# A hand-laid order of pieces and table of engines, laid anew: block-causal attention, routed attention and a gated MLP on one core

## The chip, the cores and the metric

The kernel runs on one core of one Trainium2 chip. A core has a matrix engine (TensorE, in profiles PE, with PEld for the loads of its weights), a vector engine (VectorE, DVE), a scalar engine (ScalarE, ACT), a general engine (GpSimd, POOL) and a sync engine (SyncE, SP) that mostly issues DMAs. Each engine takes its instructions from a queue of its own, in the order in which they were written, and waits at semaphores for what other engines make. The metric is the device time in microseconds (us) of one execution. Of the kernel before there are three timed runs, 936.07, 938.05 and 939.17 us, with a median of 938.05 us.

## The reference

For eight batches of 576 rows the reference runs three layers, one behind the other:

```
scores = q @ k^T / 8                     # 8 heads of 64 columns
scores = where(block_i >= block_j, scores, -1e9)      # blocks of 64
x = softmax(scores) @ v                  # (576, 512) for each batch

logits = x @ w_gate                      # 4 experts, the best 2 for each row
for e in range(4):
    q, k, v = x @ wq[e], x @ wk[e], x @ wv[e]
    a = softmax(causal(q @ k^T / 8))
    out += weight_of_e_in_this_row * (a @ v @ wo[e])

h = relu(out @ w_in)                     # 1024 columns
u, v = h[:, :512], h[:, 512:]
v_n = (v - mean(v)) / sqrt(var(v) + 1e-6)
y = (u * (w_spatial @ v_n + b_spatial)) @ w_out
```

## The kernel before, in words

**Tiles.** The 576 rows of a batch lie as four blocks of 128 rows and one of 64. Attention works on pairs of heads (four pairs a batch) or pairs of experts (two a batch), so a pair is named by batch and number: (0,4) is the first pair of experts of batch 0, (1,2) the third pair of heads of batch 1. Every matrix that TensorE multiplies is a pair of float16 tensors, a high part and what is left over, made by a cast (`copy16`, L350 to L357) or a scaled cast (`split16`, L233 to L239) and a subtraction. A product is then three matmuls.

**Steps of a pair.** *lq* and *lv* load q, k and v (L257 to L274). *mg* takes largest magnitudes for the scale (ACT L295 or DVE L297), *pq* and *pv* split q, k and v. *sc* has four parts: matmuls (L393 to L411), a row maximum (DVE L414, L416), a small step that makes the bias of the exponential (ACT L424 or DVE L426), and the exponentials (ACT L430, L435). *w* has three parts, and each casts the exponentials to float16 (ACT L352, DVE L354 or POOL L356) and subtracts (DVE L451 or POOL L455). *wt* is a transposing DMA on SP's queue (L460) that puts the result into the tile `pT`, *av* multiplies it with v on PE (L470) and takes the reciprocal of the sums (DVE L486, L488; L491 for a pair of experts), and *x* scales the product (DVE L499), casts and subtracts again (L504) and transposes (L506).

**Steps of a batch.** From x come the experts' q, k, v and logits (*proj* L804 to L817, *vproj* L827 to L836), the choice of two experts (*gate* L843 to L864, tiny DVE operations), pairs 4 and 5, and then the MLP: *hv* (L883 to L893), *norm0* and *norm* (L898 to L929), *gu* and *gs* (the two factors of the gate, L964 to L987), *outp*, *last* and *outp4* (L998 to L1027). *norm* has a part for each of five row blocks: one scales and shifts the block (L921, DVE or POOL), ACT casts it (L924, L926), and DVE or POOL subtracts (L929).

**Setting up.** Once, before batch 0 reaches its experts: *ldA* loads the experts' weights, *ldB* w_spatial and b_spatial in nine DMAs (L606 to L616), *ldwo* the matrix wo (L706), and w_in and w_out are converted, multiplied and split.

**What sets the order.** All of this is some 1,366 named steps, each a Python generator that is cut into pieces at its `yield`s. The tuple ORDER (from L1037) lists step numbers, and each appearance of a number issues the next piece of that step, on whatever engines the piece uses. So one list sets the order in all five queues at once. The table WAYS (from L1213) says for a place, and for each batch in turn (the last entry holds for the batches behind it), which engine a piece uses: D for DVE, A for ACT, G for POOL, S for SP's queue. Of two letters the first is the cast and the second the subtraction:

```
for i in ORDER:
    t = named[i]
    ...
    run(t)
```

Nothing else decides on time: waits are semaphores on data and on buffers (four double banks of PSUM, `duo`; four tiles each of `pf`, `p` and `pT`; eight of x).

## Time and profile before

| | |
|---|---|
| timed runs | 936.07, 938.05, 939.17 us, median 938.05 |
| the profiled execution | 931.44 us, its span 929.7 us |
| mean granted clock of TensorE | 0.962 |
| PE busy | 838.6 us (90%) |
| DVE busy | 754.4 us (81%) |
| ACT busy | 632.9 us (68%) |
| POOL busy | 547.5 us (59%) |

The profile is that of one execution, 6.61 us below the median of the timed runs. Busy time counts instructions that compute or, on POOL, issue DMAs. Where DVE is busy for nearly all of a stretch in which PE is not, what DVE has to do sets the pace there, and the rows of PE say in brackets how long it sat idle ahead of an instruction and what ended that.

### The profile page before, as it was taken

The numbers are of one execution on the slowest core, as the hardware profiler recorded it, in microseconds if no ns is written. First come the engines' busy times: TensorE is split into PE (matmuls) and PEld (weight loads), VectorE is DVE, ScalarE is ACT, GpSimd is POOL, SyncE is SP. The second block draws the span as 40 slices with busy tenths as digits, with TensorE's granted clock in tenths as the row PEclk, the third lists the DMA queues.
The fourth block names the chain that finished last, engine by engine and source line by source line (L and its number), as shares of the span: only waits on it lengthen the run. The fifth ranks groups of instructions, "written<-read, shape, count | busy, mean of one in ns | idle before, by whom it ended". The sixth has DMA issues, their size and how long they took to land. (4 is left out here: it accounts for less than half of the span.)

```text
span 929.7 us, 25206 instructions
## 1 busy us (share of the span) xinstructions
PE 838.6 (90%) x10038; PEld 616.4 (66%) x10038; DVE 754.4 (81%) x1608; ACT 632.9 (68%) x1151; POOL 547.5 (59%) x542
## 2 busy tenths in 40 slices
PE   3677887789998999989999999989999999999987
PEld 2466765567766767666776677567767786667554
DVE  6999989988998688887988799788997879468351
ACT  3867687866778777785776697675698568448232
POOL 6557457756677767785675867345857665425120
PEclk9777999599999999999999999999999999999999
DMA  9999889998789798999799799879699939914601
GB/s 202 217 220 191 185 178 177 193 158 133 164 152 201 112 186 149 197 189 169 137 159 197 133 149 199 145 138 181 139 180 171 158 58 155 202 30 77 140 1 57
DMA packets 470716, 143.66 MB, mean 155 GB/s; under 512 B 456003, under 2 KB 462499, under 8 KB 470598
## 3 DMA queue, kind: packets, MB, share of 16 engines
q1 hardware_dynamic: 461750, 129.72, 78.4%
q0 software_dynamic: 5232, 11.44, 4.9%
q8 instruction: 79, 1.29, 0.5%
q10 hardware_dynamic: 3616, 0.89, 0.5%
q14 instruction: 39, 0.32, 0.1%
HBM read 38.19 MB, written 9.44 MB: 51 GB/s over the span
## 5 line engine op out<-in xcount | busy, mean ns | idle before, releaser
L455 POOL TENSOR_TENSOR p<-pf,p 128x512 f16<-128x512 f32 (+1 forms) x198 | 242.5, 1247 | 74.7 <-DVE p L354 24.8
L414 DVE TENSOR_REDUCE st<-duo 128x2 f32<-128x1024 f32 (+2 forms) x192 | 151.2, 814 | 17.5 <-PE duo L401 8.8
L470 PEld LDWEIGHTS <-pT 128*128 128x128 f16 x4320 | 144.6, 99 | 28.2 <-DMA pT<-p 12.9
L435 ACT ACTIVATE pf<-duo,st,es 128x512 f32<-128x512 f32 (+3 forms) x224 | 122.4, 617 | 17.0 <-DVE st L426 14.2
L393 PE MATMUL duo<-qk 64*128 64x256 f16 (+3 forms) x1152 | 110.9, 315 | 20.6 <-DVE qk L239 7.7
L356 POOL TENSOR_SCALAR p<-pf 128x1024 f16<-128x1024 f32 (+1 forms) x68 | 78.0, 1149 | 86.5 <-ACT pf L435 55.9
L980 PE MATMUL duo<-wsp,vn 128*128 128x288 f16 x832 | 111.9, 286 | 2.1 <-ACT pf L435 1.1
L470 PE MATMUL duo<-v,pT 128*128 128x65 f16 (+1 forms) x2880 | 102.3, 196 | 10.2 <-DMA pT<-p 5.4
L804 PE MATMUL duo<-x,wqk 128*128 128x288 f16 x768 | 98.7, 286 | 2.1 <-DVE pf L499 0.7
L980 PEld LDWEIGHTS <-vn 128*128 128x128 f16 x832 | 80.0, 98 | 24.0 <-DVE vn L929 1.6
L804 PEld LDWEIGHTS <-wqk 128*128 128x128 f16 x768 | 74.3, 98 | 21.9 <-issue 2.9
L998 PE MATMUL duo<-wo,gT 128*128 128x512 f16 x384 | 86.0, 379 | 0.2 <-POOL gT L987 0.2
L393 PEld LDWEIGHTS <-qk 64*128 64x128 f16 x1152 | 46.2, 98 | 52.5 <-issue 33.0
L921 POOL TENSOR_SCALAR vf<-vf,nw 128x512 f32<-128x512 f32 (+1 forms) x27 | 25.8, 963 | 82.7 <-DVE nw L912 36.6
L435 ACT ACTIVATE pf<-duo,st,mt 128x256 f32<-128x256 f32 (+3 forms) x128 | 69.8, 617 | 5.3 <-DVE st L426 4.0
L451 DVE TENSOR_TENSOR p<-pf,p 128x1024 f16<-128x1024 f32 (+1 forms) x45 | 64.6, 1436 | 6.1 <-ACT p L352 5.8
L998 PEld LDWEIGHTS <-gT 128*128 128x128 f16 x384 | 36.6, 98 | 43.3 <-DVE gT L987 1.0
L504 POOL TENSOR_TENSOR xh<-pf,xh 128x640 f16<-128x640 f32 x30 | 44.8, 1494 | 32.9 <-ACT xh L352 26.6
L827 PE MATMUL duo<-wvg,x 128*128 128x260 f16 x480 | 56.5, 274 | 0.6 <-DVE nw L912 0.6
L352 ACT CAST p<-pf 128x1024 f16<-128x1024 f32 (+1 forms) x53 | 56.7, 1072 | 0.5
L470 PE MATMUL duo<-V,pT 128*128 128x65 f16 (+1 forms) x1440 | 49.6, 194 | 7.8 <-DMA pT<-p 5.2
L883 PE MATMUL duo<-wf,x 128*128 128x512 f16 x240 | 54.5, 379 | 1.8 <-DMA x<-xh 1.2
(273 smaller groups left out, 1732.2 us busy)
## 6 DMA issues: line engine op xcount, KB each, us to landing
out_dram<-pf SPq DMA_DIRECT2D x16, 512.0 KB, 3.3
nat<-in_q_dram SPq DMA_DIRECT2D x40, 128.0 KB, 3.2
nat<-in_k_dram SPq DMA_DIRECT2D x40, 128.0 KB, 3.2
wf<-in_moe_w_in_dram SPq DMA_DIRECT2D x8, 512.0 KB, 5.3
nat<-in_v_dram SPq DMA_DIRECT2D x32, 128.0 KB, 3.0
nat<-in_v_dram POOLq DMA_DIRECT2D x30, 128.0 KB, 4.6
nat<-in_q_dram POOLq DMA_DIRECT2D x22, 128.0 KB, 4.4
nat<-in_k_dram POOLq DMA_DIRECT2D x22, 128.0 KB, 4.4
```

The costliest lines, as they stand in the source:

```text
L352: A.copy(hi, src)
L356: G.tensor_scalar(hi, src, 1.0, 1.0, op0=OP.mult, op1=OP.mult)
L393: T.matmul(ph[:, hh, o:o + w], p.q[hs, a, ts], p.k[hs, bb, 0:w], start=i == 0, stop=False)
L414: V.reduce_max(st[:, 0, 2 * c:2 * c + 2], ph[:, :, off[c]:off[c] + P * (c + 1)], axis=AX.X)
L435: A.activation(pf[:, n * hh + off[c]:n * hh + off[c] + w], ph[:, hh, off[c]:off[c] + w], AF.Exp, bias=st[:, 1, 2 * c + hh:2 * c + hh + 1], ...
L451: V.tensor_sub(lo, src, hi)
L455: G.tensor_sub(lo[:, z:z + m], src[:, z:z + m], hi[:, z:z + m])
L470: T.matmul(ps[:, hh, o:o + n], pT[:, col(t, kk):col(t, kk) + P], p.v[:, hh, kk, a:a + n], start=kk == 0 and i == 0, stop=kk == nk - 1 and ...
L804: T.matmul(ps[:, MID + a:MID + a + w], wqk16[:, l, c, 2 * n + i, :], x16[c][:, r, a:a + w], start=m == 0, stop=m == 11)
L827: T.matmul(ps[:, i, :260], x16[d][:, l, P * c:P * c + P], wvg16[:, r, d, :], start=m == 0, stop=m == 11)
L980: T.matmul(ps[:, MID + a:MID + a + n], l, wsp16[:, r, c, a:a + n], start=i == 0, stop=i == 13)
L998: T.matmul(ps[:, i], gT[:, x, d, P * c:P * c + P], wo16[:, y, d, :], start=m == 0, stop=m == 11)
```

## The change

Only ORDER and WAYS differ. The same steps with the same operands are issued in another order, and some pieces go to another engine. Of ORDER a line tells nothing by itself (50 is a step's number):

```diff
-        50, 54, 54, 50, 51, 50, 50, 50, 54, 50, 50, 52, 142, 142, 142, 143, 143, 51, 54, 54, 143, 143, 143, 143, 54,
+        50, 54, 54, 51, 50, 50, 50, 50, 54, 50, 50, 52, 142, 142, 142, 143, 143, 51, 143, 54, 143, 143, 54, 54, 54,
...
-        "last": ("A", "G", "G", "G", "G", "G", "A", "D"), "lq.0": ("A", "S", "S", "S", "G", "S", "S", "G"),
+        "last": ("A", "G", "G", "G", "G", "G", "A", "G"), "lq.0": ("A", "S", "S", "S", "S", "S", "S", "G"),
...
-        "lq.3": ("S", "G", "S", "G", "G", "G", "S"), "lv.0": ("A", "G", "S", "S", "S", "S", "G"),
+        "lq.3": ("S", "G", "S", "G", "G", "G", "S"), "lv.0": ("A", "G", "G", "S", "G", "S", "G", "S"),
...
-        "mg.0.1": ("D", "A"), "mg.1.0": ("D", "D", "A", "A", "A", "D", "A", "D"),
+        "mg.0.1": ("A",), "mg.1.0": ("D", "D", "A", "D", "A", "D", "A", "D"),
...
-        "sc.5.3": ("D", "A", "D", "D", "A", "D", "D", "A"), "su.ldA": ("S",), "su.ldB": ("S",), "su.ldwo": ("G",),
+        "sc.5.3": ("D", "A", "D", "D", "A", "D", "A"), "su.ldA": ("S",), "su.ldB": ("G",), "su.ldwo": ("S",),
...
-        "w.4.0": ("AG", "GG", "DG", "DD", "GG", "DG", "DD", "DG"),
+        "w.4.0": ("AG", "GG", "AG", "DD", "GG", "GG", "AD", "AG"),
...
-        "x.1": ("DD", "DD", "GG", "GD", "GG", "AG", "GG", "GD"),
+        "x.1": ("DD", "GG", "GG", "GG", "GG", "AG", "GG", "AD"),
...
```

Over the whole program DVE has 1,597 instructions instead of 1,610, ACT 1,108 instead of 1,101, POOL 560 instead of 547 and SP 436 instead of 440. PE has the same 19,441, in an order in which mostly neighbours have changed places. On DVE there are 6 fewer magnitudes of a 128x640 tile (L297) and 5 fewer casts of 1,024 columns (L354).

**The start, POOL and SP.** The nine loads of *ldB* go from SP's queue to POOL's, and *ldwo* from POOL's to SP's. On POOL these rows stand behind the loads of v in the order before (the `p` rows are the casts and subtractions of pairs (0,0) and (0,1)):

```order
L274 DMA nat<-in_v_dram 64x2x64 x2
L356 TENSOR_SCALAR p_142<-pf 128x1024
L455 TENSOR_TENSOR p_142<-pf,p_142 128x512 x2
L356 TENSOR_SCALAR p_142<-pf 128x1088
L455 TENSOR_TENSOR p_142<-pf,p_142 128x544 x2
L235 TENSOR_SCALAR v<-nat,scb 128x10x64
L455 TENSOR_TENSOR p_142<-pf,p_142 128x512 x2
L706 DMA V_146<-in_moe_wo_dram 128x2x512
L455 TENSOR_TENSOR p_142<-pf,p_142 128x512 x2
```

And in the order of the change:

```order
L609 DMA wspb<-in_moe_w_spatial_dram 128x576
L356 TENSOR_SCALAR p_142<-pf 128x1024
L611 DMA wspb<-in_moe_w_spatial_dram 64x576
L455 TENSOR_TENSOR p_142<-pf,p_142 128x512 x2
L356 TENSOR_SCALAR p_142<-pf 128x1088
L455 TENSOR_TENSOR p_142<-pf,p_142 128x544 x2
L606 DMA wspa<-in_moe_w_spatial_dram 128x3x64
L609 DMA wspb<-in_moe_w_spatial_dram 128x64
L235 TENSOR_SCALAR v<-nat,scb 128x10x64
L611 DMA wspb<-in_moe_w_spatial_dram 64x64
L616 DMA wspb<-in_moe_b_spatial_dram 1x16x36 x3
L455 TENSOR_TENSOR p_142<-pf,p_142 128x512 x4
```

Four loads (L611 and three of L616) now stand between the split of v (L235) and the subtractions of pair (0,1), where there were none, the other five stand ahead of and between the pieces of pair (0,0), and L706 is gone. On SP's queue the stretch with the transposes of the first two pairs reads, before:

```order
L606 DMA wspa<-in_moe_w_spatial_dram 128x3x64
L460 DMA_TRANSPOSE pT<-p_142 128x16x128
L531 DMA wf_171<-in_moe_w_in_dram 128x4x512
L609 DMA wspb<-in_moe_w_spatial_dram 128x64
L611 DMA wspb<-in_moe_w_spatial_dram 64x64
L616 DMA wspb<-in_moe_b_spatial_dram 1x576 x2
L460 DMA_TRANSPOSE pT<-p_142 128x18x128
L616 DMA wspb<-in_moe_b_spatial_dram 1x576
L460 DMA_TRANSPOSE pT<-p_142 128x16x128 x2
L460 DMA_TRANSPOSE pT<-p_142 128x18x128
```

and in the change:

```order
L595 DMA wg<-in_moe_w_gate_dram 128x4x4
L460 DMA_TRANSPOSE pT<-p_142 128x16x128
L531 DMA wf_171<-in_moe_w_in_dram 128x4x512
L460 DMA_TRANSPOSE pT<-p_142 128x18x128
L706 DMA V_146<-in_moe_wo_dram 128x2x512
L460 DMA_TRANSPOSE pT<-p_142 128x16x128 x2
L460 DMA_TRANSPOSE pT<-p_142 128x18x128
```

The transposes of pair (0,1) no longer have loads of *ldB* between them, and one load of wo stands there in their place.

**The end of batch 0's heads, DVE and POOL.** In this stretch the last pairs of heads of batch 0, its experts' first pair (0,4) and the first pairs of batch 1 are in work together. On DVE, before (L499 is the product of *x* of pair (1,1), `xh` its cast and subtraction, `wo` the split of w_out):

```order
L499 TENSOR_TENSOR pf<-duo,rr 128x2x5x64
L451 TENSOR_TENSOR p_142<-pf,p_142 128x1088
L239 SCALAR_TENSOR_TENSOR qk<-duo,scb,qk 128x576
L414 TENSOR_REDUCE st<-duo 128x2 x2
L354 CAST xh<-pf 128x640
L857 TENSOR_REDUCE gs<-g 128x5
L414 TENSOR_REDUCE st<-duo 128x2
L239 SCALAR_TENSOR_TENSOR wo_173<-wout,scw,wo_173 128x1024
L504 TENSOR_TENSOR xh<-pf,xh 128x640
L416 TENSOR_REDUCE st<-duo 128x1
L414 TENSOR_REDUCE st<-duo 128x2
L859 TENSOR_SCALAR gs<-gs 128x5
```

and in the change:

```order
L499 TENSOR_TENSOR pf<-duo,rr 128x2x5x64
L855 SCALAR_TENSOR_TENSOR g<-g 128x20
L414 TENSOR_REDUCE st<-duo 128x2 x3
L426 TENSOR_SCALAR st<-st,mt 128x2x2
L857 TENSOR_REDUCE gs<-g 128x5
L239 SCALAR_TENSOR_TENSOR wo_173<-wout,scw,wo_173 128x1024
L416 TENSOR_REDUCE st<-duo 128x1
L859 TENSOR_SCALAR gs<-gs 128x5
L297 TENSOR_REDUCE mst<-nat 128x1
L426 TENSOR_SCALAR st<-st,mt 128x1
```

The cast and the subtraction of *x* (L354, L504) have left DVE for POOL, the small steps L426 have come from ACT, and the gate's L855 stands behind the product L499 instead of three operations ahead of it. Outside these rows, DVE also gives up the casts of the first and the third part of *w* of pair (1,3), and the casts of *x* of (1,2) and of (0,4); the first, the third and the fourth go to ACT. In all five L426 come to DVE in this stretch. POOL's queue before, in the same stretch (the `p` rows belong to pairs (0,4) and (1,3)):

```order
L261 DMA nat<-in_q_dram 64x64
L271 DMA nat<-in_v_dram 128x4x64
L274 DMA nat<-in_v_dram 64x2x64
L263 DMA nat<-in_k_dram 64x2x64
L455 TENSOR_TENSOR p_142<-pf,p_142 128x512 x2
L356 TENSOR_SCALAR p_142<-pf 128x1024
L455 TENSOR_TENSOR p_142<-pf,p_142 128x512 x2
L455 TENSOR_TENSOR p_142<-pf,p_142 128x544 x2
L455 TENSOR_TENSOR p_142<-pf,p_142 128x512 x2
L504 TENSOR_TENSOR xh<-pf,xh 128x640
L455 TENSOR_TENSOR p_142<-pf,p_142 128x512 x2
```

and in the change:

```order
L271 DMA nat<-in_v_dram 128x4x64
L263 DMA nat<-in_k_dram 64x2x64
L356 TENSOR_SCALAR xh<-pf 128x640
L504 TENSOR_TENSOR xh<-pf,xh 128x640
L274 DMA nat<-in_v_dram 64x2x64
L455 TENSOR_TENSOR p_142<-pf,p_142 128x512 x2
L356 TENSOR_SCALAR p_142<-pf 128x1024
L455 TENSOR_TENSOR p_142<-pf,p_142 128x512 x2
L455 TENSOR_TENSOR p_142<-pf,p_142 128x544 x2
L455 TENSOR_TENSOR p_142<-pf,p_142 128x512 x2
L356 TENSOR_SCALAR xh<-pf 128x640
L504 TENSOR_TENSOR xh<-pf,xh 128x640
```

The cast and subtraction of *x* of pair (1,1) now stand ahead of the subtraction of *w* of pair (0,4), and the cast of (1,2) ahead of its subtraction. The third load of v of pair (2,0), L274, is new in this queue, with its two others further up; they were on SP's.

**The end, POOL.** The last rows of POOL's queue before are *norm*, *gs* and nothing else:

```order
L356 TENSOR_SCALAR xh<-pf 128x640
L504 TENSOR_TENSOR xh<-pf,xh 128x640
L921 TENSOR_SCALAR vf<-vf,nw 128x512 x2
L929 TENSOR_TENSOR vn<-vf,vn 128x512
L987 TENSOR_TENSOR gT<-u,gT 128x576 x2
```

and in the change:

```order
L504 TENSOR_TENSOR xh<-pf,xh 128x640
L921 TENSOR_SCALAR vf<-vf,nw 128x512 x3
L929 TENSOR_TENSOR vn<-vf,vn 128x512
L987 TENSOR_TENSOR gT<-u,gT 128x576 x2
L356 TENSOR_SCALAR g_3065<-gT 128x8x64
```

L921 now runs for row blocks 0, 2 and 3 on POOL where it ran for 0 and 1, still ahead of block 0's subtraction L929; the copy of *last* has come from DVE; and the cast of `xh` in the first row is now ACT's.

## Rows read from the trace of the kernel before

**Rows 1.** Busy time by stretch (start:end, length, engines busy, PE clock, DMA share)

```profile
0.00:25.00 25.00, 10.20 (x56) 6.35 (x57) 16.60 (x70) 8.76 (x17) 16.25 (x41) 1.00 1.00 201
25.00:105.00 80.00, 60.02 (x582) 47.93 (x581) 75.98 (x155) 59.55 (x110) 47.99 (x50) 0.74 1.03 211
150.00:200.00 50.00, 34.83 (x540) 26.58 (x537) 45.44 (x82) 40.91 (x77) 32.39 (x32) 0.76 1.03 182
200.00:850.00 650.00, 623.22 (x7774) 459.11 (x7774) 541.24 (x1137) 463.31 (x849) 408.13 (x384) 1.00 0.86 152
850.00:930.00 80.00, 70.39 (x587) 44.58 (x585) 33.43 (x77) 28.15 (x42) 16.99 (x14) 0.96 0.36 76
```

**Rows 2.** Groups by line and form (busy, mean ns | idle before)

```profile
L297 DVE TENSOR_REDUCE mst<-nat 128x1 f32<-128x640 f32 x13 | 10.5, 807 | 0.0
L426 DVE TENSOR_SCALAR st<-st,mt 128x2 f32<-128x2 f32 x8 | 2.5, 309 | 0.2
L855 DVE SCALAR_TENSOR_TENSOR g<-g 128x20 f32<-128x20 f32 x8 | 4.3, 542 | 0.0
...
L504 POOL TENSOR_TENSOR xh<-pf,xh 128x640 f16<-128x640 f32 x30 | 44.8, 1494 | 32.9 <-ACT xh L352 26.6 <-DVE xh L354 5.2
L271 POOL DMA_DIRECT2D nat<-in_v_dram x30 | 23.5, 785 | 5.5 <-issue 4.0 <-DVE v L239 1.0 <-DMA nat<-in_q_dram 0.5
...
L356 POOL TENSOR_SCALAR xh<-pf 128x640 f16<-128x640 f32 x20 | 15.5, 773 | 29.7 <-DVE pf L499 16.3 <-issue 13.4
```

**Rows 3.** Timelines of POOL and SP's queue at the start (start, length, instruction [idle before])

```profile
37.65 2.26 POOL L455 TENSOR_TENSOR p<-pf,p 128x512 f16<-128x512 f32 x2
...
44.55 2.26 POOL L455 TENSOR_TENSOR p<-pf,p 128x512 f16<-128x512 f32 x2 [3.92 <-DVE p L354]
...
45.52 0.42 SPq L616 DMA_DIRECT2D wspb<-in_moe_b_spatial_dram  x1
```

**Rows 4.** Timeline of PE in the second stretch

```profile
161.67 0.83 PE L393 MATMUL duo<-qk 64*128 64x256 f16 x6 [3.60 <-DVE pf L499]
...
174.66 1.45 PE L470 MATMUL duo<-v,pT 128*128 128x65 f16 x42 [1.97 <-DMA pT<-p]
...
180.85 1.60 PE L408 MATMUL duo<-qk 128*128 128x288 f16 x6 [1.47 <-DVE neb L218]
```

**Rows 5.** Timeline of DVE in the same stretch

```profile
156.98 1.97 DVE L855 SCALAR_TENSOR_TENSOR g<-g 128x20 f32<-128x20 f32 x1
...
164.66 0.48 DVE L354 CAST xh<-pf 128x640 f16<-128x640 f32 x1
...
166.93 0.81 DVE L504 TENSOR_TENSOR xh<-pf,xh 128x640 f16<-128x640 f32 x1
...
176.72 0.67 DVE L354 CAST p<-pf 128x1024 f16<-128x1024 f32 x1
...
178.16 0.81 DVE L354 CAST xh<-pf 128x640 f16<-128x640 f32 x1
...
185.87 0.73 DVE L354 CAST p<-pf 128x1088 f16<-128x1088 f32 x1
...
194.19 0.48 DVE L354 CAST xh<-pf 128x640 f16<-128x640 f32 x1
```

**Rows 6.** Timeline of POOL in the same stretch

```profile
155.86 0.76 POOL L271 DMA_DIRECT2D nat<-in_v_dram  x1 [4.02 <-issue]
156.63 2.27 POOL L455 TENSOR_TENSOR p<-pf,p 128x512 f16<-128x512 f32 x2
...
166.59 3.29 POOL L455 TENSOR_TENSOR p<-pf,p 128x512 f16<-128x512 f32 x2 [1.83 <-ACT p L352]
```

**Rows 7.** Timeline of PE between two row products of batch 0

```profile
263.04 1.63 PE L964 MATMUL duo<-x,wf 128*128 128x288 f16 x12 [1.01 <-DVE u L982]
```

**Rows 8.** Timelines of POOL and PE at the last batch's normalization

```profile
890.42 2.84 POOL L921 TENSOR_SCALAR vf<-vf,nw 128x512 f32<-128x512 f32 x2 [20.37 <-DVE nw L912]
893.24 1.15 POOL L929 TENSOR_TENSOR vn<-vf,vn 128x512 f16<-128x512 f32 x1
...
894.45 2.17 PE L980 MATMUL duo<-wsp,vn 128*128 128x288 f16 x11 [0.50 <-POOL vn L929]
```

426 rows, old and new, of tables (ORDER, WAYS) are left out of this document.

## The prediction, made before the change was run

> **What bounds the kernel now.** I read the busy times by stretch first [rows 1], since a share over the whole span mixes stages with different limits. Of the five stretches shown PE leaves out 14.8 us of the first 25 (nothing to multiply yet), 20.0 of the next 80, 15.2 of the 50 from 150 on, 26.8 of the 650 from 200 to 850, and 9.6 of the last 80. Between 25 and 105 DVE is busy 75.98 of 80 us, so there DVE sets the pace; between 150 and 200 it is busy 45.44 of 50 and ACT 40.91. From 200 to 850 PE is busy 96% at full clock, and no change of order can gain more there than 26.8 us, spread over seven batches. So the change, which leaves PE's work as it is, can win in the two early stretches, a little all along, and can lose at the end, where every wait is on the path.
>
> Then the timeline of PE in the second stretch [rows 4]: the longest waits end on DVE's product for *x* (3.60), on the bookkeeping of a scale on DVE (1.47), and on a transposed `pT` (1.97). The first two are DVE's; the third stands at the end of a chain exponential, cast, subtraction, transposing DMA, in which POOL has a part. DVE's and POOL's timelines of the same stretch [rows 5, 6] give the price of what moves; the groups by form [rows 2] give the price of what has no row of its own there.
>
> **The start (25 to 105).** DVE loses the 128x640 maximum of pair (0,0) and that of (1,2) to ACT, 2 x 0.81 = 1.61 us [rows 2], and gains small bias steps at 0.31 apiece, of which one stands ahead of the point where batch 0's experts begin: -1.3 us there. ACT, busy 59.55 of these 80 us, covers what it takes. The nine loads of *ldB* leave SP for POOL. Nearest price on POOL: 0.79 us for a load of v [rows 2]. Four loads between the split of v and the subtraction that started at 37.65 make that at most 4 x 0.79 = 3.1 us later; what is late behind it is nothing, as POOL sat 3.92 us idle before its next subtraction, at 44.55, and SP took up that pair's transposes only after its last load at 45.52 [rows 3]. That last load, of b_spatial, goes out on POOL at about 37.65 + 3.1 = 40.8, 4.8 us earlier, and the maxima of w_spatial can start so much earlier; but they feed DVE, which has no room for them. The SP queue loses some small waits between transposes. I take -1.2. From below, if the earlier w_spatial lets DVE fill what is left of its 4.0 idle us, it is -4; from above, if the four loads and the transposes behind them come late by their whole price, +3.
>
> **The end of batch 0's heads (150 to 200).** DVE loses 0.48 + 0.81 (*x* of (1,1)), 0.67 and 0.73 (casts of *w* of (1,3)), 0.81 and 0.48 (casts of *x* of (1,2) and (0,4)), together 3.98 us [rows 5], and gains five bias steps at 0.31, 1.55 [rows 2]: -2.4 us. ACT gives those five back and takes three casts, and comes out about level. POOL gains a cast (0.77), a subtraction (1.49), another cast (0.77) and three loads of v (3 x 0.79 = 2.36): 5.4 us [rows 2]. Against that it sat idle 4.02 us before the loads at 155.86 and 1.83 before the subtraction at 166.59 [rows 6], 5.85 us, and the new pieces stand ahead of just that subtraction, so most of it falls into time that nobody used. What DVE saves shortens the waits of 3.60 and 1.47 on PE; the one of 1.97 stays, as POOL is in its chain. So I count three quarters of the 2.4: -1.8. The ends: all of DVE's saving and as much again from PE, whose mean granted clock in this stretch is 0.76 of full [rows 1] and which would lose less of it with fewer waits, -5; POOL's whole 5.4 on the path without any of DVE's gain, +5.
>
> The trace shows one thing that speaks against moving work to POOL. The gate's multiplication, 128x20, took 1.97 us at 156.98 [rows 5], while the mean of all eight is 0.54 [rows 2]; it ended at 158.95, and POOL's pair of subtractions from 156.63 to 158.90 [rows 6] covers it. The Trainium skill has a rule for this (page "SBUF — State Buffer", section "SBUF: two separate sides"): a port pair is shared by VectorE and GpSimd and held as an exclusive lock, so that one blocks for the other's whole instruction. By that rule each POOL operation that is added can cost DVE one blocked operation; the row agrees for one operation, and does not tell how often it happens. What that would make of the sum is a rival below, worked out from the rows.
>
> **From 200 to 850.** The engines of single pieces change in nearly every batch. Over the whole program that is 13 instructions fewer on DVE and 13 more on POOL (nine of them the loads at the start), which is busy 408.13 of these 650 us, so it has room. PE's queue only swaps neighbours, and the distance from a score to its *av* hardly changes, so most of the 26.8 us stays. One place can be read off: the 1.01 us before a *gu* of batch 0, ended by DVE's product for `u` [rows 7], now has matmuls of a batch 1 pair ahead of it that fill it. I take that, -1.0, and keep a fifth of the 26.8 on either side, -5 to +5, because each batch has small waits which I can't follow one by one.
>
> **The end (850 to 930).** *norm* of batch 7: POOL ran two scalings in 2.84 us and then the subtraction in 1.15, and PE's *gs* waited for that subtraction, at 894.45 [rows 8]. Now POOL runs three scalings first. A third costs 2.84 / 2 = 1.4 us at the length that they had here; DVE has one fewer beside it, so less, perhaps 1.0. No other work of PE is left to cover it. So +1.0, between 0 (if PE's order there finds another block first) and +1.4. The copy of *last* on POOL lies beside the matmuls of *outp*.
>
> **Sum.** -1.2 - 1.8 - 1.0 + 1.0 = -3.0 us, against the profiled execution's own 931.44 us: 928.4. That execution stood 6.61 us below the median of the three runs, 938.05, and I take the runs after to lie as those before: 938.05 - 3.0 = 935.0.
>
> **Rivals.**
> 1. *POOL becomes late in the second stretch.* The new cast and subtraction stand ahead of the subtraction at 166.59, and everything of pair (0,4) and (1,3) is in series behind it. If *x* of (1,1) comes from DVE no sooner than now, POOL's 5.85 idle us can't take the new pieces, since it is waiting for them. Then the chain to `pT`, which already ends PE's wait of 1.97 us [rows 4], is 5.4 later, less the 2.4 that DVE gains: +3.0, with the end's +1.0 and nothing from the other stretches +4.0, 942. Deciding point: when the last subtraction of *w* of (0,4) on POOL ends later than SP is free for its transpose. For it: POOL is busy 32.39 of 50 there and its queue is in order. Against it: the two idle times just ahead.
> 2. *Nothing that can be measured.* The waits that PE has end on chains through several engines, and what DVE drops is made up by a wait on the transposes and on ACT. Then -1.2 at the start, 0, 0 and +1.0: 937.9. For it: PE's order is nearly what it was. Against it: DVE at 95% in the first stretch.
> 3. *POOL blocks DVE.* One collision cost 1.97 - 0.33 = 1.6 us (0.33 being the mean of the other seven, (4.34 - 1.97) / 7, from the busy 4.3 and the mean 0.542 [rows 2]). Three POOL operations come into the second stretch: 3 x 1.6 = 4.9 us against the 2.4 that DVE saves, +2.5; with the start as it is and the end's +1.0, about 940.5. It is what the page's rule would make of this change. Against it: DVE's larger operations show no such stretch in most rows.
> 4. *More than I count.* DVE's whole saving arrives in both stretches with earlier w_spatial loads and PE's clock stays up: -4 - 5 - 1 + 1 = -9, 929.
>
> **How the numbers follow.** My forecast has 0.40, rival 1 0.17, rival 2 0.20, rival 3 0.10, rival 4 0.13. The forecast's own range is 931 to 938. A measurement of this kernel can tell about 0.3%, 2.8 us, from no change, so faster begins below 935.2 and slower above 940.9; the forecast lies at that edge. Of the forecast 0.26 is faster, 0.12 the same and 0.02 slower; of rival 1 0.13 slower and 0.04 the same; of rival 2 0.05 faster, 0.12 the same, 0.03 slower; of rival 3 0.05 slower and 0.05 the same; rival 4 is faster. Together 0.44 faster, 0.33 the same, 0.23 slower. The range that holds the time 8 times in 10 reaches from rival 4 with the -5 of the long stretch, 924, to rival 1 with the +3 of the start, 945.
>
> **What would show it.** In the first stretch the busy time of DVE per stretch should stay above 94% while the same work ends 1 to 2 us earlier (the first experts' matmuls earlier). In the second, the waits that end on L499 and on L218 should shrink and none should end on POOL's L455 for more than 2 us; a wait on `pT` above 4 us before an *av* of (0,4) would be rival 1. L855 or another tiny DVE operation above 1.5 us beside a POOL subtraction more than once would be rival 3. Before L980 of batch 7 PE should wait about 1.5 us instead of 0.50. I am wrong if the start is later at the first experts' matmul, or if the stretch from 200 to 850 alone moves by more than 5 us.

## The result and the profile after

The changed kernel is slower: median 947.51 us (945.68 to 949.51, four runs) against 937.33 (936.07 to 939.17, four runs) of the kernel before on the same chip, a ratio of 1.0108 with a 95% interval of 1.0074 to 1.0141. The forecast was 935.0 us, the range 924 to 945; the time lies above the range. The profiled execution took 949.51 us, with a span of 947.8 and a mean clock of 0.951. That is 18 us above the profiled execution before, where the medians are 10 apart, so the two traces hold some 8 us of chance between them. What is chance and what is not had to come from repetition; the traces of the experiments below serve for that too.

Busy time by stretch after the change (start:end, length, PE, PEld, DVE, ACT and POOL busy, PE clock, DMA share, GB/s), the rows that answer to [rows 1]:

```profile
25.00:105.00 80.00, 54.72 (x552) 43.20 (x551) 74.35 (x140) 57.24 (x106) 49.43 (x56) 0.71 1.04 196
...
150.00:200.00 50.00, 34.37 (x536) 25.14 (x532) 45.85 (x90) 43.45 (x79) 38.60 (x41) 0.86 1.11 183
200.00:850.00 650.00, 615.50 (x7664) 450.60 (x7665) 532.21 (x1108) 455.52 (x836) 399.46 (x369) 0.99 0.84 153
```

The stretches are shifted by up to 18 us against those of before, so what they contain is not the same. But in the second one DVE should have lost 2.4 us of work, and it is as busy as before (45.85 against 45.44), while POOL took 6.2 us more. The whole program says it more plainly. The first part of the page after:

```profile
PE 843.8 (89%) x10038; PEld 616.3 (65%) x10038; DVE 754.3 (80%) x1595; ACT 640.5 (68%) x1164; POOL 562.1 (59%) x555
```

DVE has 13 instructions fewer, and by the mean durations of before the difference is worth 13.8 us; its busy time is 754.3 us, as before the 754.4. Group by group (both traces by line, name and form), the operations that are left take 13.9 us longer, POOL's 1.2 and ACT's 0.5. So of these three it was DVE that was slowed. Three of the groups after the change (busy, mean ns | idle before), the answer to [rows 2]:

```profile
L426 DVE TENSOR_SCALAR st<-st,mt 128x2 f32<-128x2 f32 x8 | 6.9, 858 | 0.1
L543 DVE SCALAR_TENSOR_TENSOR x<-wf,x 128x512 int32<-128x512 int32 x4 | 6.0, 1489 | 0.1
L297 DVE TENSOR_REDUCE mst<-nat 128x1 f32<-128x640 f32 x7 | 5.6, 805 | 0.0
```

The bias step of 128x2 took 309 ns in the mean before and takes 858, for the most part by a single one of 3.32 us; the maximum L297 is not touched (807 and 805). What the slow ones have in common stands in all sixteen traces, those of the experiments below included. I held each DVE operation against the shortest twentieth of its own form in all of them: 195 are longer than that by over 1 us, and all 195 overlap an operation of POOL that computes. Those that overlap one are too long by 64.9 us together before the change and by 77.4 after it, those that overlap none by 12.0 and 11.5. The timelines of DVE and POOL at the start show the largest (start, length, instruction [idle before]):

```profile
27.36 1.46 DVE L542 SCALAR_TENSOR_TENSOR x<-wf,x 128x512 int32<-128x512 int32 x1
28.86 3.88 DVE L543 SCALAR_TENSOR_TENSOR x<-wf,x 128x512 int32<-128x512 int32 x1
```

```profile
26.75 1.54 POOL L356 TENSOR_SCALAR p<-pf 128x1024 f16<-128x1024 f32 x1 [5.53 <-ACT pf L435]
28.25 0.58 POOL L611 DMA_DIRECT2D wspb<-in_moe_w_spatial_dram  x1
28.86 2.27 POOL L455 TENSOR_TENSOR p<-pf,p 128x512 f16<-128x512 f32 x2
31.10 1.09 POOL L356 TENSOR_SCALAR p<-pf 128x1088 f16<-128x1088 f32 x1
32.28 2.71 POOL L455 TENSOR_TENSOR p<-pf,p 128x544 f16<-128x544 f32 x2
```

L543 started with POOL's pair of subtractions and ended only after the cast behind it, 3.88 us for work that takes 0.69 where POOL is idle. In the order before, L542 and L543 stand later, at 34.80 and 35.51, where POOL was between two pieces. Behind them DVE had PE's operand for pair (0,1), and PE waited for it. PE's timeline there, after and before:

```profile
33.69 1.67 PE L393 MATMUL duo<-qk 64*128 64x512 f16 x6 [6.15 <-DVE qk L239]
```

```profile
29.86 1.67 PE L393 MATMUL duo<-qk 64*128 64x512 f16 x6 [2.17 <-ACT pf L430]
```

The second place lies in batch 2, in the long stretch that I had called safe. PE's timeline after the change (L211 are the two small matmuls of the MLP's scale, L804 is batch 3's projection):

```profile
441.73 0.38 PE L211 MATMUL duo<-dgh,ones 1*128 1x1 f32 x2
...
445.59 4.77 PE L804 MATMUL duo<-x,wqk 128*128 128x288 f16 x24 [3.02 <-DVE neh L218]
```

And the same projection before the change:

```profile
433.69 3.10 PE L804 MATMUL duo<-x,wqk 128*128 128x288 f16 x24 [0.34 <-DVE neh L218]
```

The projection needs a PSUM buffer that L218 on DVE gives back. DVE's timeline after the change shows what L218 now stands behind, and the one before what it stood behind there:

```profile
442.30 1.27 DVE L891 BATCH_NORM_STATS2 bs<-vf 128x6 f32<-128x512 f32 x2
443.49 0.30 DVE L893 BATCH_NORM_AGGREGATE mv<-bs 128x2 f32<-128x6 f32 x2
443.70 1.25 DVE L414 TENSOR_REDUCE st<-duo 128x2 f32<-128x768 f32 x2
444.88 0.61 DVE L898 TENSOR_SCALAR nw<-mv 128x5 f32<-128x5 f32 x1
445.39 0.14 DVE L218 TENSOR_SCALAR neh<-duo 128x1 int32<-128x1 int32 x1
```

```profile
432.34 1.23 DVE L414 TENSOR_REDUCE st<-duo 128x2 f32<-128x1024 f32 x1 [0.97 <-PE duo L403]
433.49 0.15 DVE L218 TENSOR_SCALAR neh<-duo 128x1 int32<-128x1 int32 x1
```

Hardly anything here is slow. An operation of 0.14 us that gives back a buffer stands 3 us further down a queue. And the wait is paid twice: the 24 matmuls behind it took 4.77 us instead of 3.10. Two stretches of the change's trace, the wait with the short matmuls ahead of it and the 24 matmuls (columns as above), show why:

```profile
441.00:445.50 4.50, 1.57 (x30) 1.15 (x25) 4.40 (x10) 2.72 (x6) 1.05 (x1) 1.00 0.95 190
445.60:450.20 4.60, 4.60 (x24) 3.08 (x24) 4.36 (x16) 1.80 (x4) 2.55 (x2) 0.63 0.67 146
```

PE is busy through the second, at a granted clock of 0.63: most of it at the lower of the two levels (1.2 GHz), the rest at the full one.

The third is in batch 4. DVE's gate subtraction of 128x20 elements, POOL beside it, and the same subtraction before the change:

```profile
550.77 2.06 DVE L851 TENSOR_TENSOR g<-lg,gs 128x20 f32<-128x20 f32 x1
```

```profile
550.51 2.29 POOL L455 TENSOR_TENSOR p<-pf,p 128x512 f16<-128x512 f32 x2
```

```profile
532.25 1.06 DVE L851 TENSOR_TENSOR g<-lg,gs 128x20 f32<-128x20 f32 x1
```

At the end of the program the rows that answer to [rows 8], of POOL and then of PE:

```profile
907.93 3.26 POOL L921 TENSOR_SCALAR vf<-vf,nw 128x512 f32<-128x512 f32 x3 [21.15 <-DVE nw L912]
911.15 1.67 POOL L929 TENSOR_TENSOR vn<-vf,vn 128x512 f16<-128x512 f32 x1
```

```profile
912.88 1.56 PE L980 MATMUL duo<-wsp,vn 128*128 128x288 f16 x11 [1.24 <-POOL vn L929]
```

PE's wait grew from 0.50 to 1.24 us.

To find the rest, I took from each trace the time at which PE starts the first projection of each batch. The table has the first start and the distances to the next ones, in us, each from one execution; the labels are those of the experiments below. "Old" and "new" tell the order in the stretch.

| trace | to batch 0 | 0 to 1 | 1 to 2 | 2 to 3 | 3 to 4 | 4 to 5 | 5 to 6 | 6 to 7 |
|---|---|---|---|---|---|---|---|---|
| before (old) | 119.5 | 82.4 | 106.5 | 105.4 | 94.9 | 106.9 | 93.5 | 101.0 |
| after (new) | 125.2 | 85.8 | 106.3 | 105.5 | 98.6 | 110.3 | 94.3 | 102.2 |
| e1 (old to batch 0, new) | 119.3 | 80.7 | 107.2 | 105.5 | 98.2 | 110.2 | 96.8 | 101.6 |
| e7 (old, new 0 to 3, old) | 124.2 | 83.2 | 106.7 | 105.4 | 95.6 | 109.2 | 95.7 | 101.0 |
| e8 (new, two moved) | 123.0 | 84.0 | 106.4 | 105.4 | 94.6 | 110.1 | 94.6 | 102.4 |
| e9 (new, three moved) | 120.9 | 81.0 | 105.8 | 105.4 | 94.1 | 109.3 | 95.8 | 102.1 |
| e14 (old, two put in) | 122.5 | 86.9 | 106.4 | 105.9 | 102.0 | 106.9 | 93.9 | 101.3 |

The first two columns differ by 4 to 5 us between executions with the same order there (119.3 in e1, 124.2 in e7): in that stretch waits on DMA loads differ from one execution to the next (POOL waited 9.5 us for loads of v in e7 and 0.4 in e1). From batch 1 on most stretches repeat within 1 us, those from 4 to 6 within 3, and the new order loses in 3 to 4 (some 3.5 us), in 4 to 5 (some 3), and a little in 5 to 7. The row of e7 has 109.2 in 4 to 5 with the old order there; its profiled execution, 942.75 us, was the slowest of its twelve (median 935.96).

### The profile page after: what moved, and what is told of

Read it like the earlier page. It is cut to its first block, busy times and chain, and to the rows that moved or that the text cites. A ratio compares the mean times of both kernels' runs of the same rounds, so it can differ in the third digit from the quotient of the medians.

```text
span 947.8 us, 25225 instructions
## 1 busy us (share of the span) xinstructions
PE 843.8 (89%) x10038; PEld 616.3 (65%) x10038; DVE 754.3 (80%) x1595; ACT 640.5 (68%) x1164; POOL 562.1 (59%) x555
## 4 chain that ended last, share of the span: by engine, by line
PE 37%; DVE 12%; DMA 4%; ACT 3%; issue 3%; POOL 1%; SPq 0%; DVEq 0%; ACTq 0%; POOLq 0%
PE duo L980 7%; PE duo L804 5%; PE duo L470 5%; PE duo L998 5%; DMA pT<-p 3%; PE duo L883 3%; PE duo L827 3%; DVE st L414 3%; PE duo L393 3%; PE duo L964 3%; DVE p L451 2%; PE duo L408 1%; PE duo L345 1%; ACT pf L435 1%; PE duo L1020 1%
## 5 line engine op out<-in xcount | busy, mean ns | idle before, releaser
L455 POOL TENSOR_TENSOR p<-pf,p 128x512 f16<-128x512 f32 (+1 forms) x204 | 250.4, 1252 | 38.8 <-ACT p L352 17.9
L414 DVE TENSOR_REDUCE st<-duo 128x2 f32<-128x1024 f32 (+2 forms) x192 | 151.0, 814 | 17.3 <-PE duo L403 9.0
L356 POOL TENSOR_SCALAR p<-pf 128x1024 f16<-128x1024 f32 (+1 forms) x74 | 84.4, 1142 | 121.8 <-ACT pf L435 89.7
L393 PE MATMUL duo<-qk 64*128 64x256 f16 (+3 forms) x1152 | 113.3, 322 | 23.9 <-DVE qk L239 17.6
L435 ACT ACTIVATE pf<-duo,st,es 128x512 f32<-128x512 f32 (+2 forms) x224 | 122.9, 617 | 14.0 <-DVE st L426 5.2
L804 PE MATMUL duo<-x,wqk 128*128 128x288 f16 x768 | 101.7, 292 | 4.9 <-DVE neh L218 3.3
L804 PEld LDWEIGHTS <-wqk 128*128 128x128 f16 x768 | 75.8, 100 | 26.5 <-issue 5.6
L504 POOL TENSOR_TENSOR xh<-pf,xh 128x640 f16<-128x640 f32 x30 | 42.9, 1430 | 58.0 <-ACT xh L352 35.2
L921 POOL TENSOR_SCALAR vf<-vf,nw 128x512 f32<-128x512 f32 (+1 forms) x26 | 23.2, 900 | 80.5 <-DVE nw L912 43.6
L451 DVE TENSOR_TENSOR p<-pf,p 128x1024 f16<-128x1024 f32 (+1 forms) x42 | 56.3, 1341 | 0.5 <-ACT p L352 0.3
L239 DVE SCALAR_TENSOR_TENSOR qk<-duo,scb,qk 128x640 f16<-128x640 f32 (+1 forms) x56 | 46.6, 843 | 11.8 <-ACT qk L233 11.7
```

Source lines behind the costliest of these rows:

```text
L356: G.tensor_scalar(hi, src, 1.0, 1.0, op0=OP.mult, op1=OP.mult)
L393: T.matmul(ph[:, hh, o:o + w], p.q[hs, a, ts], p.k[hs, bb, 0:w], start=i == 0, stop=False)
L414: V.reduce_max(st[:, 0, 2 * c:2 * c + 2], ph[:, :, off[c]:off[c] + P * (c + 1)], axis=AX.X)
L435: A.activation(pf[:, n * hh + off[c]:n * hh + off[c] + w], ph[:, hh, off[c]:off[c] + w], AF.Exp, bias=st[:, 1, 2 * c + hh:2 * c + hh + 1], ...
L451: V.tensor_sub(lo, src, hi)
L455: G.tensor_sub(lo[:, z:z + m], src[:, z:z + m], hi[:, z:z + m])
```

## The experiments

Each time is compared with the kernel before on the same chip, whose median lay between 935.3 and 937.3 us, so the ratios count, and among them the change's own 1.0108. A ratio is estimated from all runs of both kernels and is not that of the two medians; the two differ by up to 0.2%. The kernels were made by moving entries of ORDER. The notation `hsc.2 #1` is the second piece of step hsc of batch 2.

**e1, the old start.**

```diff
-ORDER = NEW
+ORDER = OLD[:480] + (NEW without the pieces that are in OLD[:480])
+WAYS: the old entry for each step that begins in OLD[:480]
```

> The changed kernel, but its first 480 pieces (all that comes before batch 0's experts) in the order and on the engines of the kernel before; the rest is issued as the change has it. In the traces batch 0's experts begin 5.7 us later after the change (125.2 against 119.5). Theory A (each stretch's loss stays until the end): 947.5 - 5.7 = about 942, and the experts begin at 119 to 120. Theory B (what is lost at the start is caught up later, or is noise between executions): 946 to 948.

942.96 us, ratio 1.0081 (1.0060 to 1.0102), and the experts began at 119.3. Between the two theories: a quarter of the loss would go with the start, some 2.5 us and not the 5.7 of the traces, but the intervals of e1 and of the change overlap, so that this run alone shows neither a gain nor none. The trace then has the same losses as the change from batch 3 on.

**e2, the old order up to the first MLP matmul of batch 0.**

```diff
-ORDER = NEW
+ORDER = OLD[:900] + (NEW without the pieces that are in OLD[:900])
```

> The changed kernel, but its first 900 pieces (up to the first MLP matmul of batch 0) as in the kernel before. In the traces half of the loss (9.0 of 18 us) has come by then, the other half comes in batches 2 to 6. Theory A (the later batches have losses of their own): about halfway, 942 to 943. Theory B (all of the loss is made in the two early stretches, and the rest of the difference between the traces is chance): 937 to 938. Theory C (the early part is not the cause): 947.

940.33 us, ratio 1.0071 (1.0046 to 1.0096). Theory A: two thirds of the loss lie behind batch 0. In the stretch 3 to 4 it took 99.1 us, in 4 to 5 109.6, as the change.

**e3, the first conversion later.**

```diff
 w.(0,0).1 #1, s2o.(0,1) #5,
-su.win.0 #3,
 ...
 s2.0 #0,
+su.win.0 #3,
```

> The changed kernel with one piece moved: the two integer operations of the first conversion of w_in on DVE (L542, L543) come after the scale's bookkeeping of batch 0, where the kernel before has them, and no longer beside POOL's casts and subtractions of pair (0,0), where they took 1.46 and 3.88 us instead of 0.67 and 0.69. Theory A (DVE was held up by POOL's operations, 4 us, and PE behind it, 6.15 us of waiting for L239): batch 0's experts begin 2 to 4 us earlier, 944 to 945. Theory B (DVE is short of time there anyway, another operation is held up in place of these): no change, 947.

941.20 us, ratio 1.0078 (1.0052 to 1.0104), 0.3% below the change. DVE's timeline in this kernel, where POOL was between two subtractions:

```profile
34.27 0.67 DVE L542 SCALAR_TENSOR_TENSOR x<-wf,x 128x512 int32<-128x512 int32 x1
34.98 0.69 DVE L543 SCALAR_TENSOR_TENSOR x<-wf,x 128x512 int32<-128x512 int32 x1
```

1.36 us for both instead of 5.34, and the experts began at 119.4, 5.8 us earlier than in the change. Theory A, as large as expected, though the intervals of the two ratios overlap. The traces of all kernels but e10 and e11 say it with more weight: where L542 and L543 stand early (the change, e4, e5, e6, e14) the experts begin at 122.5 to 126.4, in the mean 124.6, and where they stand late (the nine others) at 119.3 to 124.2, in the mean 120.8.

**e4, the loads back on SP.**

```diff
-"su.ldB": ("G",), "su.ldwo": ("S",)
+"su.ldB": ("S",), "su.ldwo": ("G",)
```

> The changed kernel with the nine loads of w_spatial and b_spatial back on SP's queue and the load of wo back on POOL's, all else as changed. Theory A (the loads on POOL keep its queue from the casts of pair (0,1) and so cost time): 2 to 3 us less, 945. Theory B (they fall into idle time of POOL): 947 to 948, no difference; on SP they stand between the transposes again, which could even cost 1 us.

944.40 us, ratio 1.0097 (1.0072 to 1.0122): 0.1% below the change, within both intervals. That does not exclude theory A, whose 945 is a ratio of 1.0082; but the experts began at 124.7 with the loads back on SP, as in the change (125.2). No effect of the loads, to which I gave most of my attention at the start, can be told.

**e5, the MLP's scale of batch 2 earlier.**

```diff
 sc.(4,2).0 #1,
+hsc.2 #0,
 sc.(4,2).1 #0,
+hsc.2 #1,
 hv.2.1 #2,
-hsc.2 #0,
 sc.(4,2).1 #1, norm0.2 #0, ...
-hsc.2 #1,
```

> The changed kernel with two pieces moved in batch 2: the two small matmuls of the MLP's scale (L211) and the first DVE operation on them (L218), which gives their PSUM buffer back, come ahead of the second part of a score and of a statistic (L891), as in the kernel before. In the change's trace L218 stands behind 1.27 us of L891, 0.30 of L893, 1.25 of L414 and 0.61 of L898, the next projection on PE waits 3.02 us for it, and its 24 matmuls then take 4.77 us instead of 3.10 at a lower granted clock. Theory A (losses of single places add up): 3 to 4.5 us less than the change, about 941.5 on the chip where the kernel before takes 935.3. Theory B (the wait closes again, since PE then waits elsewhere): less than 1 us, 945.

942.90 us, ratio 1.0065 (1.0039 to 1.0092), 0.43% below the change: theory A, with intervals that overlap in part. PE's projection in this kernel, without a wait and at full clock (a granted clock of 1.00 from 442.7 to 445.9):

```profile
442.73 3.11 PE L804 MATMUL duo<-x,wqk 128*128 128x288 f16 x24
```

**e6, the conversion early in the old kernel.**

```diff
 w.(0,0).1 #1,
+su.win.0 #3,
 ...
 s2.0 #0,
-su.win.0 #3,
```

> The kernel before with one piece moved the other way: the two integer operations of the first conversion (L542, L543) go up to where the change has them, beside POOL's casts and subtractions of pair (0,0). Theory A (POOL's operations hold them up, and that costs the change its late start): L542 and L543 take 4 us or more instead of 1.4, and the time is 2 to 4 us above the kernel before, 938 to 939. Theory B (it is a matter of the whole new order at the start): within 1 us of the kernel before.

938.36 us, ratio 1.0027 (0.9999 to 1.0054). L542 and L543 took 1.52 us each, 3.04 instead of 1.36, less than the 4 us that I expected. Here POOL stood still for DVE too: its pair of subtractions beside L543 took 3.02 us instead of 2.27. POOL, and then PE, which now waits for L239 as in the change:

```profile
29.42 3.02 POOL L455 TENSOR_TENSOR p<-pf,p 128x512 f16<-128x512 f32 x2
```

```profile
33.22 1.67 PE L393 MATMUL duo<-qk 64*128 64x512 f16 x6 [4.89 <-DVE qk L239]
```

The time is about as theory A has it, though the interval touches no change.

**e7, the new order only in the middle.**

```diff
-ORDER = OLD
+ORDER = OLD[:480] + NEW up to proj.3.0.0 + the rest of OLD
```

> The kernel before up to batch 0's experts (480 pieces), then the change's order and engines up to the first projection of batch 3, then the kernel before again. In the trace of the first experiment this stretch ended 0.9 us earlier against the kernel before than it began, with its best point 1.8 us ahead at batch 1's experts. Theory A (the change is good for 1 to 2 us between 120 and 410 us and all its loss lies outside): 0.5 to 1.5 us below the kernel before, 934 to 935. Theory B (moving work to POOL costs there too): above the kernel before.

935.96 us, ratio 0.9988 (0.9965 to 1.0011). Between 120 and 410 us the new order costs 0.11% at most; that it gains something is not shown.

**e8, both moves.**

```diff
 (the moves of e3 and of e5 in the changed kernel)
```

> The changed kernel with both moves: the first conversion later (third experiment) and the MLP scale of batch 2 earlier (fifth). Theory A (independent places): the sum of the two gains, 4 + 4 = 8 us below the change, 937 to 938. Theory B (the second gain comes only as far as PE is not held elsewhere): about 941, as with the first move alone.

941.62 us, ratio 1.0056 (1.0033 to 1.0079): 0.52% below the change, with some 0.4% either way when both intervals are taken together, where the single gains add up to 0.73%. Between the theories, and within the intervals either could be. The two places are about half of the loss: 0.56% is left without them.

**e9, the gate's subtraction of batch 4 earlier too.**

```diff
 gate.4 #0,
+gate.4 #1,
 ...
 hmax.3 #3,
-gate.4 #1,
```

> The kernel of the eighth experiment (conversion later, MLP scale of batch 2 earlier) with a third piece moved: the gate's 128x20 subtraction of batch 4 (L851) goes up, directly behind the gate's first piece, where POOL stands idle. In all traces of the new order it took 1.8 to 2.4 us at its present place, beside a pair of POOL subtractions (L455), against 0.17 where no POOL operation runs. Theory A (DVE is blocked for the length of POOL's operation, and PE waits behind it): L851 of batch 4 takes below 0.5 us, and the stretch from batch 4's to batch 5's projection, 110.2 us in the eighth experiment, becomes 108 to 109; the time falls by 1 to 2 us. Theory B (the next DVE operation is blocked instead): L851 is short, the stretch stays at 110.

937.61 us, ratio 1.0024 (0.9991 to 1.0056): no longer to be told from the kernel before. But not by the mechanism alone that I named. L851 took 1.10 us instead of 2.06, as much as in the kernel before (1.06) and not below 0.5, because another POOL operation met it at the new place; DVE and POOL in this kernel:

```profile
530.08 1.10 DVE L851 TENSOR_TENSOR g<-lg,gs 128x20 f32<-128x20 f32 x1
```

```profile
530.03 1.11 POOL L356 TENSOR_SCALAR p<-pf 128x1088 f16<-128x1088 f32 x1
```

The stretch 4 to 5 fell by 0.8 us, to 109.3, just short of the 108 to 109 of theory A. One wait of PE is gone from it: ahead of the two L211 in it PE waited for L817 on DVE, 0.82 us in the change and 0.54 to 1.14 in e1 to e5 and e8, where L851 stands as in the change, and less than 0.5 here. The 0.3% between e8 and e9 is more than that and may be chance in part.

**e10 and e11, order and table crossed.**

```diff
 e10: ORDER as changed
-     WAYS as changed
+     WAYS of the kernel before
 e11: ORDER of the kernel before
-     WAYS of the kernel before
+     WAYS as changed
```

> The change's order of pieces (ORDER) with the table of engines (WAYS) of the kernel before. Theory A (the order is what costs: operations that DVE shares a stretch with POOL in, and buffers given back late): about as slow as the change, ratio to the kernel before 1.007 to 1.011. Theory B (the work that went to POOL is what costs): ratio 1.000 to 1.004. Each order was made for its own table, so it may also come out slower than both, above 1.011.

> The order of the kernel before with the change's table of engines. Theory A (the order costs): ratio to the kernel before 0.998 to 1.004. Theory B (the engines cost, since POOL's added work blocks DVE): 1.006 to 1.011. As before it may come out worse than either, because order and table were made for each other.

991.95 us, ratio 1.0591 (1.0552 to 1.0630), and 985.50 us, ratio 1.0523 (1.0483 to 1.0562). Both theories fall, for the question was badly put: with 136 of some 1,366 steps on an engine for which the order was not laid, the loss is five times that of the change. Order and table can't be judged apart by this pair.

**e12, what the traces showed to be good.**

```diff
-ORDER = OLD
+ORDER = OLD[:480] + (NEW with the moves of e3 and e5) up to proj.4.0.0 + the rest of OLD
```

> The kernel before up to batch 0's experts (480 pieces), then the change's order and engines with the MLP scale of batch 2 moved ahead, up to the first projection of batch 4, then the kernel before again: the stretches in which the traces show the new order level or ahead, without those in which it loses. In the trace of the three moved pieces the four stretches between the projections of batches 0 and 4 took 81.0, 105.8, 105.4 and 94.1 us against 82.4, 106.5, 105.4 and 94.9 in the kernel before, 2.9 us less. Theory A (these gains are the order's and stay): ratio to the kernel before 0.996 to 0.998. Theory B (they are of the size of what one execution differs from the next): 0.999 to 1.002.

935.87 us, ratio 1.0006 (0.9985 to 1.0027). Theory B: the advantages that I read off single traces were no larger than their chance. No version was found that beats the kernel before.

**e13 and e14, the places put into the old kernel.**

```diff
 e13: sc.(4,2).0 #1, ... sc.(4,2).1 #0,
+     hsc.2 #0,
      sc.(4,2).1 #1,
+     hsc.2 #1,
      (both taken from where they stood, ten and five pieces earlier)
 e14: the same, and su.win.0 #3 as in e6
```

> The kernel before with one thing of the change put into it: in batch 2 the first DVE operation of the MLP's scale (L218), and the two matmuls ahead of it, come behind the statistics L891 and the second maximum L414, as the change has them. Theory A (this place alone costs what the fifth experiment won back, 0.3 to 0.45%): ratio to the kernel before 1.003 to 1.005, the next projection's first matmul waits 2 to 4 us and the matmuls behind it run at a lower granted clock. Theory B (it costs only together with the rest of the new order): within 0.1% of the kernel before.

> The kernel before with both places of the change put into it: the scale of batch 2 late, and the first conversion (L542, L543) early, beside POOL's casts. Theory A (single places add up, 0.27% from the sixth experiment and 0.3 to 0.45%): ratio 1.005 to 1.008, more than half of what the change lost. Theory B (waits that are opened in different stretches close again by the end): 1.003 or less.

940.95 us, ratio 1.0040 (1.0020 to 1.0061), and 945.10 us, ratio 1.0089 (1.0060 to 1.0119). Theory A in both, e14 a little above its 1.005 to 1.008. PE's timeline of e13 shows the same pair of prices as in the change:

```profile
441.64 4.77 PE L804 MATMUL duo<-x,wqk 128*128 128x288 f16 x24 [3.53 <-DVE neh L218]
```

Three entries out of 3,671, at two places, make the old kernel 0.89% slower, and the change made it 1.08% slower. That does not make them nearly all of the change's loss, since without them (e8) it keeps 0.56%, about half. That the place in batch 2 costs time is shown by e13, whose interval lies above no change, and by its traces: the wait stands in all five kernels that have the new order there with nothing moved (3.02 us in the change and in e1 to e4) and in e13 and e14 (3.53 in both), and in no other trace but that of e10, whose order is the new one. That the conversion costs time is shown by e14 against e13 on the same chip, which differ in it alone: 4.15 us between the medians, 4.2 with an interval of 2.5 to 5.8 between the means. The single steps e3, e5 and e6 have the same signs and sizes, but the intervals of e3 and e5 overlap the change's, and that of e6 reaches no change.

## Why the prediction was wrong

**The step that failed** is the one on the long stretch: "PE's queue only swaps neighbours, and the distance from a score to its *av* hardly changes, so most of the 26.8 us stays", with -1.0 us. From batch 1's projection to batch 7's the trace after has 617.2 us (211.0 to 828.2), the one before 608.3, so this term measured +8.9 (616.7 to 619.5 in e1, e3 and e4 against 610.4 in e6). Of the 8.9 us the stretch 3 to 4, where L218 stands, has 3.7, and 4 to 7 has 5.3 without a single place that explains it. Both signs that I had set for being wrong came: the experts' first matmul was later, and this stretch moved by more than 5 us. I read the order of PE, which waits, and not that of DVE, for which it waits. DVE's busy share there left room, but an engine with room still works in order: L218 behind 3.4 us of other work is late whatever the share. The place could have been read blind, as the rows of L891, L414 and L218 in both orders, with their durations from the trace; [rows 7] was such a place, and I looked for one that gained.

**The start** was to gain 1.2 us. No cost of the loads on POOL can be told (e4), as I had argued. What cost was an edit that I had not priced, L542 and L543 moved up beside POOL's casts. e3 and e6 put that at 0.3%, some 2.5 to 3 us, and e14 against e13 at 4.2. The whole of the start, as e1 has it, is 0.27% of the change's 1.08%, with an interval of some 0.4% either way.

**Rival 3 named the mechanism and missed the place.** I had L855 at 1.97 us against 0.33 [rows 2, 5] and made of it a price for the three POOL operations that came into the second stretch, with a chance of 0.10. L855 itself is well after the change (all eight together 2.2 us instead of 4.3), since its neighbours moved. The sign that I had named for this rival, a tiny DVE operation above 1.5 us beside a POOL subtraction more than once, came true with L426 (3.32) and L851 (2.06). The collisions came where the order changed the pairing, at L543, at a bias step in batch 2, at L851, and DVE lost by such collisions about all the 13.8 us that it had been relieved of. That POOL's work and DVE's stretch go together over the whole program is read from the traces and was not tried by itself. Nor is that sum what the time went by: in e9 the operations of DVE beside POOL are too long by 75.9 us together, nearly as in the change (77.4), and its time is close to that of before. It counts where PE waits behind them; that L542 and L543 are slow beside POOL and cost the start is shown by e14 against e13. The rule that I cited from the Trainium skill (page "SBUF — State Buffer", section "SBUF: two separate sides") agrees with those rows in that DVE stands still, but not in how long: it speaks of the other's whole instruction, and L543 stood through three of POOL's in a row. I could have seen that before the change: in [rows 5, 6] L855 stood through the rest of one subtraction and the whole of the next, and I read it as agreeing.

**The second stretch** was to gain 1.8 us. With the new order the stretch from batch 0's to batch 1's projection took 80.6 to 85.8 us in nine traces (after, e1, e3 to e5, e7 to e9, e12), in the mean 82.7, and with the old 82.1 to 86.9 in five (before, e2, e6, e13, e14), in the mean 84.4. So a gain of that size is likely but not shown; e7 bounds it, from 0.35% less to 0.11% more for all of batches 0 to 2. The waits did not shrink as I had said. Beside the 3.60 us on L499 I had left out one of 1.98 on L239 ahead of it, and with the new order the two became one of 5.07 or 5.08 on L239 in all nine. PE before and after:

```profile
157.12 0.66 PE L393 MATMUL duo<-qk 64*128 64x384 f16 x6 [1.98 <-DVE qk L239]
```

```profile
166.09 1.04 PE L393 MATMUL duo<-qk 64*128 64x384 f16 x6 [5.08 <-DVE qk L239]
```

Rival 1 was half right. An *av* in the stretch waited for POOL's subtraction, for 1.4 to 3.1 us in eight of the nine, in seven of them for more than the 2 us that I had named as a sign against the forecast; in the change's own trace the wait there is 4.09 us, at 176.82, and nothing that the profile shows ended it. PE in e1:

```profile
168.55 1.28 PE L470 MATMUL duo<-v,pT 128*128 128x65 f16 x24 [2.98 <-POOL p L455]
```

A later *av* waited 2.90 us for `pT`, at 201.38 in the change's trace. Both are of pairs of heads, and the wait above 4 us before an *av* of (0,4), the sign that I had set for rival 1, did not come.

**The end** was to lose 1.0 us. PE's wait grew by 0.74 us, the third scaling costing 1.09 (3.26 / 3), but from batch 7's projection to the end the traces have 119.5 us before and 119.6 after. So the mechanism was right and its price was made up nearby.

**The scale of the sum.** Two slips in it change nothing: the other seven of L855 have a mean of 0.34, not 0.33, and the lower bound of 924 counts the long stretch's -1.0 twice. I summed four terms with bounds of up to 5 us each and let them stand for some hundreds of moved pieces. The largest term had the weakest reading, one wait of 1.01 us out of 26.8.

What stays open: the loss in batches 4 to 7. From batch 4's projection to batch 7's the eight traces with the new order there (after, e1 to e5, e8, e9) have 304.9 to 308.6 us, the five with the old (before, e6, e12 to e14) 301.5 to 302.2. These some 5 us are of the size of what e8 keeps of the loss (0.56%). They are no single wait: PE stands idle 14.7 to 17.6 us there instead of 10.3 to 11.8, in waits of 2.3 us at most, and of these only the one behind L851 was tried. How much of the 0.3% between e8 and e9 is the moved gate stays open too.

## What to carry to other kernels

When an order is laid anew, read for each wait of the busy engine the queue of the engine that ends it, and look first for the small operations that give a buffer back: every instruction that the new order puts ahead of one is on the path. Where DVE and POOL work side by side, price a DVE operation by what POOL does in the same microseconds, not by its mean; moving work from DVE to POOL can give back, as DVE's busy time, all that it takes. And of two profiles of one execution each, believe only the stretches that a third one repeats.

## What was not expected of the hardware

A DVE operation that meets POOL can wait for more than one POOL instruction: L543 of 0.69 us took 3.88, through 2.27 us of subtractions and the 1.09 us cast that was issued behind them, and a bias step of 128x2 took 3.32 us at 392.43, through three of four subtractions in a row (4.50 us from 391.16). DVE and POOL there:

```profile
392.43 3.32 DVE L426 TENSOR_SCALAR st<-st,mt 128x2 f32<-128x2 f32 x1
```

```profile
391.16 4.50 POOL L455 TENSOR_TENSOR p<-pf,p 128x512 f16<-128x512 f32 x4
```

It befell operations of 2 elements a partition as well as of 512. It is not always DVE that stands: in e6 the same two operations took 1.52 us each, and POOL's pair beside them 3.02 instead of 2.27.

After a wait of PE of 3.0 to 3.5 us the next 24 matmuls took 4.77 us instead of 3.10, in the change and in e13 alike, at a granted clock of 0.63 in both: about half as much again as the wait itself.
